# Moving two thirds of the float64 weight conversions from the expert stage into the gated passes of a fused attention, expert and gated-network kernel

## The chip, the cores and the metric

The kernel runs on one core of a Trainium2 chip. The metric is the device time of one execution in microseconds (us). The engines of the core are named as the profile names them: PE (TensorE, matrix products), DVE (VectorE), ACT (ScalarE), POOL (GpSimd) and SP (SyncE, which only issues DMAs here). Each works through its own instructions in order, and semaphores tie them together.

## The reference

Attention over eight batches of eight heads in two directions (x reads the state, the state reads x) gives 8 x 544 = 4352 tokens of width 512. A router with capacity 544 assigns each token to one of eight experts, greedily over all sorted logits. Each expert is relu(x w1) w2 with 1024 hidden columns. A gated network follows.

```python
logits = x @ w_gate
order = np.argsort(-logits.flatten())      # greedy, at most N // E tokens per expert
for e in range(E):
    mask = assigned == e
    h = np.maximum(x[mask] @ w1[e], 0.0)
    out[mask] = h @ w2[e]
...
g = x @ w_gate                             # moe2: 512 x 1536
silu = g * (1.0 / (1.0 + np.exp(-g)))
val = x @ w_val                            # moe2: 512 x 1536
return (silu * val @ w_out).astype(np.float32)   # moe2: 1536 x 512
```

The three weights of the gated network, w_gate, w_val and w_out, arrive as float64.

## The kernel before

Four stages follow one another: attention with the first search of the router (0 to about 188 us), the experts (to about 690), two gated passes (to about 1207) and the output products (to the end). All large products are made of float32 values that are split in two parts, hi (rounded, by ACT) and lo (the rest, by DVE), and each product takes the three combinations that matter.

**Experts.** There are 128 units u, 16 per expert: two parts of its 544 tokens (matmuls of 256 and of 288 columns) times eight blocks of hidden columns. A unit is `hidden` (L789: 12 matmuls into a bank h, then relu on ACT at L802 and its rest on DVE at L803) and, one unit later, `expert_out` (L806: 12 matmuls, L813, L814, L817). The weights of the next expert come meanwhile: four DMAs of 512 KB for w1 (L734) and four for w2 (L739) on SP's queue, then split on ACT (L725) and DVE (L726). The router's search for the next expert runs in between, as a chain of small DVE and PE instructions. What is done ahead of which unit is written out by hand: `at(u, hook, f, ...)` puts a call in front of unit u, and a hook places the instructions of that call behind a named instruction on that instruction's engine only. The hooks 'h' and 'hh' are the last L803 (DVE) and the last L802 (ACT).

**Conversions.** Float64 weights become float32 in 36 steps. `load64(n)` (L158) brings 512 KB of raw float64 into a buffer raw64 (two buffers), with ACT issuing the DMA (L167). `convert(n)` (L170) is one ACT multiply (L175) into mag, three DVE instructions (L177, L178, L180) into f32v and a store of 256 KB to v_d (L181, SP). Step n stands for (j, q, u): six blocks j of hidden columns, q = gate, val, out, and two halves u. All 36 stand in the experts (L991): the load in front of unit 10 + 3.2 n, behind hook 'hh', the conversion 3 units later, with hook 'h'.

**Gated passes.** The gated products are made by a seven-product scheme over 2x2 blocks (the order of the products is PORDER = 1, 6, 7, 5, 2, 4, 3). Operands are sums and differences of blocks: POOL makes four of them per operand (`s_sums` L860, `t_sums` L870, instructions L864 to L867 and L876 to L879, tiles tt out of six buffers), and ACT and DVE split them (`split`, L841 and L842). With a key, `keep` (L849) stores the four sums in DRAM, and a later call with that key loads them (`kept`, L854). Each of the two passes p goes over nine groups n of tokens (index 4 is a small group of leftovers), three units jj each (L1159). A unit has 84 matmuls (L1044; 48 in the small group), reads out of banks b1 to b4 (two buffers each) by ACT (L1075) and DVE (L1078 and others), gating (L1051 to L1053), and a store of m (L1096). A pass needs the split weights of three blocks j. In pass 0, further work is written behind units of the groups: the sums of w3, w4, w5 (`pair_load`, `pair_sums`) and of w_out o0, o1, o2 (`out_load`, `out_sums`), stored for later. In pass 1 the first six sums of activations (`acts_load`, `acts_sums`, keys a0 to a5, EARLY = 6) are made and stored.

**Output.** 27 steps, each a seven-product update with w_out (L1231); the sums of the next step's activations are loaded if they were stored, or made on POOL.

Of the kernel before, what the change touches and what calls it, by code (L numbers as in the profile page):

```python
# [21 lines left out]
F32 = mybir.dt.float32  # L22
# [3 lines left out]
I32 = mybir.dt.int32  # L26
# [9 lines left out]
E = 8  # L36
# [5 lines left out]
NT = 5  # L42
NW = 24
NY = (8, 6)
EARLY = 6
P_ = {'spin': 12, 'xl': 2, 'pc': (0, 9), 'ct': 12, 'cuts': (0, 34), 'lead': [0, 1, 10, 25, 44, 57, 73, 89], 'hook': ['p', 'p', 'p', 'p', 'p', 'x', 'p', 'p'], 'w': [8, 14, 8, 8, 8, 8, 8, 8], 'whook': 'h', 'g': [0, 3, 18, 36, 56, 70, 85, 103], 'gs': 0.34, 't': [0, 14, 29, 46, 61, 75, 91, 104], 'ts': 1, 'ghook': 'p', 'thook': None, 't0': (2, 4, 5), 'l0': 10, 'lp': 3.2, 'cd': 3, 'lhook': 'hh', 'chook': 'h', 'swap': [], 'y0': 16, 'f0': [10, 4, 3]}
PRE = 24
HEAD = "z0 m0 f0 p l z1 m1 x0 x3 x2 e0 f1 x1 e1 q"
ORDER = "z0 f0 p t0 t1 z1 G l m0 f1 x0 m1 r0 x1 s0 e0 r1 x2 x3 r2 s1 k e1 c q r3"
# [8 lines left out]
def moe_kernel(ctx: ExitStack, tc: tile.TileContext, x, state, moe_w_gate, moe_w1, moe_w2,  # L58
               moe2_w_gate, moe2_w_val, moe2_w_out, out):
    nc = tc.nc  # L60
# [64 lines left out]
    for q in range(2):  # L125
        pair = []
        for part in "hl":
            t = ac.tile([128, 4, 128], FR, name=f"SB{part}{q}")
# [3 lines left out]
    for q in range(3):  # L132
        pair = []
        for part in "hl":
            t = ac.tile([128, 2, 4, ROW], FR, name=f"RB{part}{q}")
# [19 lines left out]

    raw64 = {}

    def load64(n):  # L158
        j, q, u = n // 6, n // 2 % 3, n % 2
        src = (moe2_w_gate, moe2_w_val, moe2_w_out)[q]  # L160
        if q < 2:
            src_u = src[256 * u:256 * u + 256, 256 * j:256 * j + 256]
        else:
            src_u = src[256 * j + 128 * u:256 * j + 128 * u + 128]
        k = 2 if q < 2 else 1
        raw64[n] = bw.tile([128, 512, 2], I32, name="raw64", bufs=2)
        nc.scalar.dma_start(raw64[n].rearrange("p (k f) w -> p k (f w)", k=k),  # L167
                            src_u.bitcast(I32).rearrange("(k p) f -> p k f", p=128))

    def convert(n):  # L170
        j, q, u = n // 6, n // 2 % 3, n % 2
        raw = raw64.pop(n)
        low, top = raw[:, :, 0], raw[:, :, 1]
        mag = bw.tile([128, 512], F32, name="mag", bufs=1)
        nc.scalar.mul(mag, top.bitcast(F32), 2.0 ** -112)  # L175
        v = bw.tile([128, 512], I32, name="f32v", bufs=1)
        nc.vector.tensor_scalar(v, low, 29, None, op0=OP.logical_shift_right)  # L177
        nc.vector.scalar_tensor_tensor(v, mag.bitcast(I32), 3, v,  # L178
                                       op0=OP.logical_shift_left, op1=OP.bitwise_or)
        nc.vector.scalar_tensor_tensor(v, top, -2**31, v, op0=OP.bitwise_and, op1=OP.bitwise_or)  # L180
        nc.sync.dma_start(v_d[j, q][:, u], f32(v))  # L181
# [411 lines left out]
    for b in range(B + 1):  # L593
        steps = ORDER if 0 < b < B else HEAD if b == 0 else TAIL
        for op in steps.split():
            k, q = op[0], int(op[1:] or 0)
# [243 lines left out]
    def split(hi, lo, src):  # L840
        nc.scalar.copy(hi, src)  # L841
        nc.vector.tensor_tensor(lo, src, f32(hi), OP.subtract)  # L842

    def tmp(pool):
        return pool.tile([128, 2, 256], F32, name="tt", bufs=4 if pool is bw else 6)

# [39 lines left out]
    def pair_load(j, pool):  # L886
        if pool is bw:
            raws = [pool.tile([128, 1024], F32, name="raw", bufs=4) for _ in range(2)]
        else:
            raw = pool.tile([128, 2048], F32, name="raw", bufs=2)  # L890
            raws = [raw[:, :1024], raw[:, 1024:]]
        for q in range(2):
            nc.sync.dma_start(raws[q], v_d[j, q].rearrange("p u f -> p (u f)"))
        if pool is bw:
            parts = [r.rearrange("p (q u k f) -> p q u k f", q=1, u=2, k=2) for r in raws]
        else:
            parts = [raw.rearrange("p (q u k f) -> p q u k f", q=2, u=2, k=2)]
        return [[v[:, :, u, :, 128 * i:128 * i + 128] for i in range(2) for u in range(2)] for v in parts]

    def pair_sums(A, pool, key=None):  # L900
        cut = [lambda t, q=q: t.rearrange("p q (k f) -> p q k f", k=2)[:, q:q + 3 - len(A)] for q in range(len(A))]
        if key in sums_d:
            S1, S2, S3, S4 = kept(key, pool)
        else:
            S1, S2, S3, S4 = S = s_sums(A, pool, cut)
            if key:
                keep(key, S)
        whole = lambda t: [c(t) for c in cut]
        return {1: [a[0] for a in A], 6: whole(S2), 7: whole(S3), 2: [a[1] for a in A],
                5: whole(S1), 4: [a[3] for a in A], 3: whole(S4)}  # L910
# [77 lines left out]
            at(P_["t"][k] + int(j * P_["ts"]), P_["thook"], turn, k, j)  # L988
    for j in range(2, NT):
        at(P_["t0"][j - 2], "p", turn, 0, j)  # L990
    for n in range(36):  # L991
        at(int(P_["l0"] + P_["lp"] * n), P_["lhook"], load64, n)
        at(int(P_["l0"] + P_["lp"] * n + P_["cd"]), P_["chook"], convert, n)

    pend = None
    for u in range(16 * E):
        i, hf, f = u // 16, u // 8 % 2, u % 8
# [105 lines left out]
    def acts_load(gi, jj):  # L1103
        n = 4 if gi < E else 2
        raw = cw.tile([128, 2048], F32, name="raw", bufs=2)[:, :512 * n].rearrange("p (r i t) -> p r i t", r=2, i=n)
        nc.sync.dma_start(raw, m_d[gi][:, 2 * jj:2 * jj + 2])
        return raw

    def acts_sums(gi, raw, key=None):
        if gi < E:  # L1110
            a11, a21, a12, a22 = (raw[:, :, i] for i in range(4))
            if key in sums_d:
                S1, S2, S3, S4 = kept(key, cw)
            else:
                S1, S2, S3, S4 = S = s_sums([(a11, a12, a21, a22)], cw, [lambda t: t])
                if key:
                    keep(key, S)
            return {1: a11, 6: S2, 7: S3, 2: a12, 5: S1, 4: a22, 3: S4}
        a1, a2 = raw[:, :, 0], raw[:, :, 1]
        t, neg = tmp(cw), tmp(cw)  # L1120
        nc.gpsimd.tensor_tensor(t, a1, a2, OP.add)
        nc.gpsimd.tensor_scalar(neg, a1, -1.0, None, op0=OP.mult)
        return {1: a1, 2: a2, 3: t, 7: neg}
# [6 lines left out]
    def out_load(jj):  # L1130
        raw = cw.tile([128, 2048], F32, name="raw", bufs=2).rearrange("p (r i f) -> p r i f", r=2, i=2)
        for r in range(2):
            nc.sync.dma_start(raw[:, r], v_d[2 * jj + r, 2])
        return raw

    def out_sums(jj, raw):
        return t_sums([raw[:, :, i, 256 * d:256 * d + 256] for i in range(2) for d in range(2)], cw, f"o{jj}")
# [21 lines left out]
    for p, n, gi, jj in hidden_units:  # L1159
        nxt = groups[p][n + 1] if n < E else None  # L1160
        if jj == (p == n == 0) and nxt is not None:
            ysrc = y_sums(nxt, y_load(nxt, cw), cw)

        def after(step):
            if nxt is None or (gi == E) != (step < 3 and gi == E):
                return
            if gi == E:
                todo = {(0, 1): (0, 1), (0, 2): (1, 2), (1, 1): (2, 3), (1, 2): (3, 4), (2, 1): (4, 5), (2, 2): (5, 7)}
                a, b = todo[jj, step]
                todo = PORDER[a:b]  # L1170
            else:
                todo = {(1, 1): (1,), (1, 7): (6,), (1, 5): (7,), (2, 1): (5,), (2, 6): (2,), (2, 2): (4,),
                        (2, 5): (3,)}.get((jj, step), ())
            for m in todo:
                if m in ysrc:
                    y_combo((p, nxt), m, ysrc)

        if n == E and p == 0 and jj == 0:
            wraw = pair_load(3, cw)
        unit(key, 3 * p + jj, gi, after)  # L1180
        if p == 1 and 2 <= n < 2 + EARLY and n < E:
            if jj == 1:
                early = acts_load(*outs[n - 2])
            elif jj == 2:
                acts_sums(outs[n - 2][0], early, f"a{n - 2}")
        if p == 0 and 1 <= n < 7 and jj == 1:
            early = pair_load(n + 2, cw) if n < 4 else out_load(n - 4)
        if p == 0 and 1 <= n < 7 and jj == 2:
            if n < 4:
                pair_sums(early, cw, f"w{n + 2}")  # L1190
            else:
                out_sums(n - 4, early)
        if n == E and p == 0:
            src = pair_sums(wraw, cw, f"w{3 + jj}")
            if jj < 2:
                wraw = pair_load(4 + jj, cw)
            for m in PORDER:
                pair_combo(3 + jj, m, src)
        if n == E and p == 1:
            src = out_sums(jj, out_load(jj))  # L1200
            for m in PORDER:
                out_combo(jj, m, src)
            if jj == 1:
                acts[0] = acts_sums(outs[0][0], acts_load(*outs[0]), "a0")
                acts_prep(0, slice(0, 7))
        if jj == 2 and nxt is not None:
            key = (p, nxt)
        elif jj == 2 and p == 0:
            key = (0, gi)
# [101 lines left out]
```

## Time and profile before

| | us |
|---|---|
| median of three runs | 1485.01 |
| lowest and highest | 1481.55, 1488.06 |
| the profiled execution | 1485.12 |
| its span, first to last instruction | 1483.5 |
| PE busy (matmuls) | 1384.4 |
| DVE busy | 1126.4 |
| ACT busy | 571.0 |
| POOL busy | 468.2 |

Busy times are those of the profiled execution. Matmuls are pipelined, so a PE that is busy all the time can still wait a little inside. Views used below: the chain of work that ended last, busy times of each engine in given stretches, waits of an engine by what ended them, and instructions in order of time. The granted clock is the share of full speed that TensorE was given in a stretch; it has two levels, 1.0 (2.4 GHz) and 0.5 (1.2 GHz).

### The profile page before, as it was taken

To read this page: it belongs to the slowest core of one execution; us is meant where nothing else is said; L and a number is where in the kernel's file an instruction comes from. 1 tells how busy PE (TensorE), PEld (TensorE's weight loads), DVE (VectorE), ACT (ScalarE), POOL (GpSimd) and SP (SyncE) were. 2 spreads that over 40 slices of the span, in tenths; PEclk is the share of its full clock that TensorE was granted. 3 is DMA by queue.
4 is the path that set the end of the run, shared out by engine and by line. 5 is a ranking of instruction groups with operands and counts; after the bars stand their busy time and mean duration, and the time that the engine had idled before them with its cause. 6 is when DMAs were issued, how large, how long until landed. Compare 5 with 4: busy or idle time off the path is not lost.

```text
span 1483.5 us, 29094 instructions
## 1 busy us (share of the span) xinstructions
PE 1384.4 (93%) x11440; PEld 1335.4 (90%) x11441; DVE 1126.4 (76%) x2152; ACT 571.0 (38%) x1124; POOL 468.2 (32%) x398
## 2 busy tenths in 40 slices
PE   6998389998999999999999999999999999999997
PEld 5776278988988899999999999999999999999996
DVE  5898768876777765586888677976856797999982
ACT  5885124332332333343323232522323264444441
POOL 4775331100111001152553410012131002778872
PEclk9999579999999999999999999999999999999999
DMA  7542225545444356455665553635465378334431
GB/s 129 124 113 91 97 77 192 188 155 192 147 163 160 126 197 213 164 181 199 225 237 192 192 185 115 234 143 192 173 213 204 129 246 294 119 138 144 151 118 43
DMA packets 125417, 244.67 MB, mean 165 GB/s; under 512 B 48096, under 2 KB 57312, under 8 KB 118624
## 3 DMA queue, kind: packets, MB, share of 16 engines
q1 hardware_dynamic: 107696, 203.46, 40.6%
q10 hardware_dynamic: 11472, 19.43, 4.2%
q0 software_dynamic: 6112, 19.93, 3.9%
q8 instruction: 89, 1.46, 0.4%
q14 instruction: 48, 0.39, 0.1%
HBM read 157.84 MB, written 84.93 MB: 164 GB/s over the span
## 4 chain that ended last, share of the span: by engine, by line
PE 71%; DVE 11%; DMA 8%; issue 4%; ACT 3%; POOL 2%; SPq 0%; POOLq 0%; DVEq 0%; ACTq 0%
PE b L1044 44%; PE h L798 11%; PE y L817 4%; PE y L813 4%; PE y L814 3%; DMA raw<-in_moe_w_out_dram 2%; DMA raw<-v_d 1%; DMA raw<-in_moe_w_gate_dram 1%; DMA raw<-in_moe_w_val_dram 1%; DVE w L726 1%; PE bt L777 1%; DMA xc<-in_x_dram 1%; DVE xw L320 1%; DVE yb L842 1%; DMA raw<-in_moe_w_dram 1%
## 5 line engine op out<-in xcount | busy, mean ns | idle before, releaser
L1044 PE MATMUL b<-yb,w 128*128 128x256 f32 x4320 | 517.5, 282 | 6.9 <-DVE cs L1084 5.7
L1044 PEld LDWEIGHTS b<-yb,w 128*128 128x128 f32 x4320 | 515.0, 190 | 9.3 <-DVE cs L1084 7.2
L1044 PE MATMUL b<-w,yb 128*128 128x256 f32 x2160 | 257.2, 282 | 0.0
L1044 PEld LDWEIGHTS b<-w,yb 128*128 128x128 f32 x2160 | 257.0, 190 | 0.0
L798 PE MATMUL h<-xh,w 128*128 128x288 f32 (+1 forms) x1024 | 215.4, 303 | 0.7 <-issue 0.7
L798 PEld LDWEIGHTS h<-xh,w 128*128 128x128 f32 x1024 | 167.8, 197 | 1.7 <-issue 1.1
L768 POOL DMA_INDIRECT xg<-xm_d,idx x38 | 48.1, 1265 | 367.8 <-PE bt L777 163.4
L842 DVE TENSOR_TENSOR yb<-tt,yb 128x512 fp32r<-128x512 f32 x164 | 143.7, 893 | 14.4 <-ACT yb L841 14.4
L813 PE MATMUL y<-hh,w 128*128 128x288 f32 (+1 forms) x512 | 140.2, 300 | 12.6 <-DVE ys L825 4.8
L798 PE MATMUL h<-xl,w 128*128 128x288 f32 (+1 forms) x512 | 151.9, 299 | 0.0
L841 ACT CAST yb<-tt 128x512 fp32r<-128x512 f32 x164 | 101.2, 620 | 104.6 <-PE b L1044 87.8
L814 PE MATMUL y<-hh,w 128*128 128x288 f32 (+1 forms) x512 | 139.2, 298 | 0.0
L842 DVE TENSOR_TENSOR yb<-raw,yb 128x512 fp32r<-128x512 f32 x127 | 126.0, 1000 | 15.8 <-ACT yb L841 13.5
L864 POOL TENSOR_TENSOR tt<-raw 128x512 f32<-128x512 f32 (+1 forms) x33 | 42.0, 1277 | 286.9 <-DMA raw<-m_d 212.9
L802 ACT ACTIVATE hh<-h 128x288 fp32r<-128x288 f32 (+1 forms) x128 | 50.7, 397 | 199.2 <-PE h L798 177.5
L813 PEld LDWEIGHTS y<-hh,w 128*128 128x128 f32 x512 | 98.7, 194 | 14.9 <-ACT ys L823 6.3
L803 DVE SCALAR_TENSOR_TENSOR hl<-h,hh 128x288 fp32r<-128x288 f32 (+1 forms) x128 | 55.5, 435 | 69.6 <-ACT hh L802 63.7
L841 ACT CAST yb<-raw 128x512 fp32r<-128x512 f32 x127 | 78.1, 620 | 63.5 <-PE b L1044 50.2
L798 PEld LDWEIGHTS h<-xl,w 128*128 128x128 f32 x512 | 99.5, 196 | 0.2
L814 PEld LDWEIGHTS y<-hh,w 128*128 128x128 f32 x512 | 98.7, 194 | 0.3
L817 PE MATMUL y<-hl,w 128*128 128x288 f32 (+1 forms) x512 | 94.9, 300 | 2.2 <-DVE hl L803 2.2
L726 DVE TENSOR_TENSOR w<-raw,w 128x1024 fp32r<-128x1024 f32 x61 | 73.8, 1238 | 16.1 <-ACT w L725 15.4
(253 smaller groups left out, 2107.7 us busy)
## 6 DMA issues: line engine op xcount, KB each, us to landing
raw<-in_moe_w_dram SPq DMA_DIRECT2D x60, 512.0 KB
raw<-m_d SPq DMA_DIRECT2D x30, 1024.0 KB
m_d<-m SPq DMA_DIRECT2D x48, 512.0 KB
raw<-v_d SPq DMA_DIRECT2D x32, 512.0 KB
raw<-y_d SPq DMA_DIRECT2D x14, 1024.0 KB
v_d<-f32v SPq DMA_DIRECT2D x36, 256.0 KB
xm_d<-xm SPq DMA_DIRECT2D x8, 1024.0 KB
y_d<-ys SPq DMA_DIRECT2D x16, 512.0 KB
```

The source lines that it names most:

```text
L726: eng.tensor_tensor(lo, raw, f32(hi), OP.subtract)
L768: hooks["g"] = nc.gpsimd.indirect_dma_start(out=xg[:n], out_offset=None, in_=xm_d, in_offset=bass.IndirectOffsetOnAxis(ap=idx[i][:n, j:j + ...
L798: hooks["p"] = nc.tensor.matmul(ph, W[i][0][k][q == 1][:, fs], (xl if q == 2 else xh)[:, k, :T], start=(n == 0), stop=(n == 11)).ins
L802: relu[16 * i + 8 * hf + f] = hooks["hh"] = nc.scalar.activation(hh, ph, AF.Relu).ins
L803: hooks["h"] = nc.vector.scalar_tensor_tensor(hl, ph, 0.0, f32(hh), op0=OP.max, op1=OP.subtract).ins
L813: nc.tensor.matmul(p[d], wh[:, f % 2, ds_], hh, start=(f == 0), stop=False)
L814: nc.tensor.matmul(p[d], wl[:, f % 2, ds_], hh, start=False, stop=False)
L817: nc.tensor.matmul(p[d], wh[:, f % 2, ds_], hl, start=False, stop=(f == 7))
L841: nc.scalar.copy(hi, src)
L842: nc.vector.tensor_tensor(lo, src, f32(hi), OP.subtract)
L864: nc.gpsimd.tensor_tensor(S1, a21, a22, OP.add)
L1044: nc.tensor.matmul(p[:, q], a(x, q), b(y), skip_group_check=True, start=start and not (q or n or m), stop=stop and q == 1 and n == last an ...
```

## The change

The order of the 36 conversions becomes a list CONV: first the 12 for the gate and val weights of j = 0 to 2, then the 12 for those of j = 3 to 5, then the 12 for w_out. The experts keep the first 12, one every 8.4 units, each conversion 6 units behind its load. The second 12 are written into pass 0, the third into pass 1: with group n the load of one behind unit 0, the load of a second and the conversion of the first behind unit 1, the conversion of the second behind unit 2, in six groups of each pass (n = 0, 1, 2, 3, 5, 6). Their loads are issued by SP, raw64 there has one buffer, and mag and f32v are taken from the six tt buffers. The sums of w3, w4, w5 move from groups 1, 2, 3 of pass 0 to groups 2, 5, 7; those of w_out from groups 4, 5, 6 of pass 0 to groups 2, 5, 7 of pass 1. Of the activations' sums four are made ahead and stored instead of six, at groups 1, 3, 4, 6 of pass 1.

```diff
-EARLY = 6
-P_ = {..., 'lp': 3.2, 'cd': 3, ...}
+EARLY = 4
+P_ = {..., 'lp': 8.4, 'cd': 6, ...}
...
-    def load64(n):
-        j, q, u = n // 6, n // 2 % 3, n % 2
+    CONV = ([(j, q, u) for j in range(3) for q in range(2) for u in range(2)]
+            + [(j, q, u) for j in range(3, 6) for q in range(2) for u in range(2)]
+            + [(j, 2, u) for j in range(6) for u in range(2)])
+
+    def load64(n, pool=None, eng=nc.scalar):
+        j, q, u = CONV[n]
...
-        raw64[n] = bw.tile([128, 512, 2], I32, name="raw64", bufs=2)
-        nc.scalar.dma_start(raw64[n].rearrange("p (k f) w -> p k (f w)", k=k),
+        raw64[n] = (pool or bw).tile([128, 512, 2], I32, name="raw64", bufs=1 if pool else 2)
+        eng.dma_start(raw64[n].rearrange("p (k f) w -> p k (f w)", k=k),
...
-    def convert(n):
-        j, q, u = n // 6, n // 2 % 3, n % 2
+    def convert(n, pool=None):
+        j, q, u = CONV[n]
...
-        mag = bw.tile([128, 512], F32, name="mag", bufs=1)
+        mag = bw.tile([128, 512], F32, name="mag", bufs=1) if pool is None else flat(tmp(pool))
...
-        v = bw.tile([128, 512], I32, name="f32v", bufs=1)
+        v = bw.tile([128, 512], I32, name="f32v", bufs=1) if pool is None else flat(tmp(pool)).bitcast(I32)
...
-    for n in range(36):
+    for n in range(12):
         at(int(P_["l0"] + P_["lp"] * n), P_["lhook"], load64, n)
         at(int(P_["l0"] + P_["lp"] * n + P_["cd"]), P_["chook"], convert, n)
...
         unit(key, 3 * p + jj, gi, after)
-        if p == 1 and 2 <= n < 2 + EARLY and n < E:
+        a = {1: 0, 3: 1, 4: 2, 6: 3}.get(n) if p else None
+        if a is not None:
             if jj == 1:
-                early = acts_load(*outs[n - 2])
+                early = acts_load(*outs[a])
             elif jj == 2:
-                acts_sums(outs[n - 2][0], early, f"a{n - 2}")
-        if p == 0 and 1 <= n < 7 and jj == 1:
-            early = pair_load(n + 2, cw) if n < 4 else out_load(n - 4)
-        if p == 0 and 1 <= n < 7 and jj == 2:
-            if n < 4:
-                pair_sums(early, cw, f"w{n + 2}")
+                acts_sums(outs[a][0], early, f"a{a}")
+        c = 12 + 12 * p + 2 * (0, 1, 2, 3, 9, 4, 5, 9, 9)[n]
+        if c < 24 + 12 * p:
+            if jj < 2:
+                load64(c + jj, cw, nc.sync)
+            if jj:
+                convert(c + jj - 1, cw)
+        k = {2: 0, 5: 1, 7: 2}.get(n)
+        if k is not None and jj == 1:
+            early2 = out_load(k) if p else pair_load(3 + k, cw)
+        if k is not None and jj == 2:
+            if p:
+                out_sums(k, early2)
             else:
-                out_sums(n - 4, early)
+                pair_sums(early2, cw, f"w{3 + k}")
```

## Rows read from the trace of the kernel before

**Rows 1.** The chain that ended last, shares of the span by engine and line.

```profile
PE b L1044 44%; PE h L798 11%; PE y L817 4%; PE y L813 4%; PE y L814 3%; DMA raw<-in_moe_w_out_dram 2%; DMA raw<-v_d 1%; DMA raw<-in_moe_w_gate_dram 1%; DMA raw<-in_moe_w_val_dram 1%; DVE w L726 1%; PE bt L777 1%; DMA xc<-in_x_dram 1%; DVE xw L320 1%; DVE yb L842 1%; DMA raw<-in_moe_w_dram 1%
```

**Rows 2.** Stretches: length, busy PE, PEld, DVE, ACT, POOL, clock, DMA share, GB/s.

```profile
244.00:690.00 446.00, 421.79 (x3682) 403.56 (x3683) 322.88 (x802) 155.09 (x300) 66.24 (x60) 0.97 0.51 169
690.00:720.00 30.00, 26.75 (x214) 26.48 (x213) 20.88 (x34) 14.49 (x26) 14.41 (x8) 0.94 0.68 246
720.00:840.00 120.00, 118.42 (x994) 117.81 (x993) 98.37 (x138) 36.58 (x65) 54.12 (x38) 1.00 0.59 214
840.00:950.00 110.00, 108.84 (x908) 107.90 (x908) 83.34 (x128) 37.25 (x66) 12.89 (x9) 1.00 0.47 166
950.00:1207.00 257.00, 256.11 (x2154) 255.71 (x2153) 192.02 (x302) 86.00 (x154) 34.37 (x25) 1.00 0.53 185
...
1244.00:1470.00 226.00, 226.00 (x1903) 226.00 (x1902) 188.36 (x200) 95.01 (x155) 162.70 (x110) 1.00 0.38 131
```

**Rows 3.** Waits of ACT from 244 to 690: total us, times, longest us.

```profile
ACT mag L175 <- DMA raw<-in_moe_w_val_dram: 21.6, 7, 8.0
ACT mag L175 <- DMA raw<-in_moe_w_out_dram: 18.4, 9, 4.7
...
ACT mag L175 <- DMA raw<-in_moe_w_gate_dram: 13.6, 5, 5.9
```

**Rows 4.** ACT in order of time, 417 to 432: start, duration, instruction, [idle before].

```profile
420.76 0.37 ACTq L167 DMA_DIRECT2D raw<-in_moe_w_val_dram  x1
429.20 0.66 ACT L175 ACTIVATE mag<-raw 128x512 f32<-128x512 f32 x1 [8.03 <-DMA raw<-in_moe_w_val_dram]
429.76 0.40 ACT L802 ACTIVATE hh<-h 128x288 fp32r<-128x288 f32 x1
```

**Rows 5.** SP's DMA issues in order of time, same stretch.

```profile
418.12 4.04 SPq L739 DMA_DIRECT2D raw<-in_moe_w_dram  x4
```

**Rows 6.** One stretch of 2 us while these transfers run, columns as in rows 2.

```profile
426.00:428.00 2.00, 2.00 (x25) 1.74 (x24) 0.65 (x2) 0.00 (x0) 0.00 (x0) 1.00 1.01 373
```

**Rows 7.** Stretches around nine idle times of PE in the experts, and their sum.

```profile
302.00:306.00 4.00, 3.00 (x32) 2.76 (x31) 2.51 (x6) 2.40 (x4) 1.07 (x1) 1.00 0.81 249
338.00:342.00 4.00, 2.61 (x22) 2.40 (x21) 0.64 (x5) 0.86 (x3) 2.90 (x3) 1.00 0.90 298
363.00:376.00 13.00, 10.47 (x95) 9.49 (x93) 5.51 (x14) 3.36 (x5) 0.00 (x0) 0.74 0.34 114
...
616.00:625.00 9.00, 6.63 (x40) 6.05 (x39) 2.94 (x5) 2.96 (x6) 0.00 (x0) 0.81 0.47 168
...
sum 72.00, PE 52.60 PEld 48.45 DVE 32.24 ACT 22.25 POOL 10.01; mean PE 5.84 PEld 5.38 DVE 3.58 ACT 2.47 POOL 1.11
```

**Rows 8.** A conversion's DVE instructions: duration ns min/median/max, first and last start.

```profile
L177 DVE TENSOR_SCALAR f32v<-raw x36: 413/419/1158, 250.8 to 679.6; 128x512 int32<-128x512 int32 x36
L178 DVE SCALAR_TENSOR_TENSOR f32v<-mag,f32v x36: 669/685/1660, 251.3 to 680.2; 128x512 int32<-128x512 int32 x36
L180 DVE SCALAR_TENSOR_TENSOR f32v<-raw,f32v x36: 668/688/1111, 252.6 to 681.2; 128x512 int32<-128x512 int32 x36
```

**Rows 9.** Groups by line: count, busy us, mean ns, idle before and its releasers.

```profile
L842 DVE TENSOR_TENSOR yb<-tt,yb 128x512 fp32r<-128x512 f32 x164 | 143.7, 893 | 14.4 <-ACT yb L841 14.4
...
L1078 DVE TENSOR_TENSOR u<-b,s 128x512 f32<-128x512 f32 x48 | 32.8, 684 | 4.0 <-PE b L1044 3.5
```

**Rows 10.** SP and ACT in order of time, 722 to 790, one row each.

```profile
736.71 1.59 SPq L893 DMA_DIRECT2D raw<-v_d  x2
...
768.39 0.58 ACT L1075 COPY s<-b 128x512 f32<-128x512 f32 x1
```

**Rows 11.** From the chain (start, us, what) and from PE in time.

```profile
697.32 7.95 DMA raw<-y_d
...
715.05 1.20 PE L1044 MATMUL b<-yb,w 128*128 128x256 f32 x8 [3.25 <-DVE cs L1084]
```

More of the change, by code (lines that the diff above doesn't have):

```diff
@@ L44 @@
 NY = (8, 6)
-EARLY = 6
-P_ = {'spin': 12, 'xl': 2, 'pc': (0, 9), 'ct': 12, 'cuts': (0, 34), 'lead': [0, 1, 10, 25, 44, 57, 73, 89], 'hook': ['p', 'p', 'p', 'p', 'p', 'x', 'p', 'p'], 'w': [8, 14, 8, 8, 8, 8, 8, 8], 'whook': 'h', 'g': [0, 3, 18, 36, 56, 70, 85, 103], 'gs': 0.34, 't': [0, 14, 29, 46, 61, 75, 91, 104], 'ts': 1, 'ghook': 'p', 'thook': None, 't0': (2, 4, 5), 'l0': 10, 'lp': 3.2, 'cd': 3, 'lhook': 'hh', 'chook': 'h', 'swap': [], 'y0': 16, 'f0': [10, 4, 3]}
+EARLY = 4
+P_ = {'spin': 12, 'xl': 2, 'pc': (0, 9), 'ct': 12, 'cuts': (0, 34), 'lead': [0, 1, 10, 25, 44, 57, 73, 89], 'hook': ['p', 'p', 'p', 'p', 'p', 'x', 'p', 'p'], 'w': [8, 14, 8, 8, 8, 8, 8, 8], 'whook': 'h', 'g': [0, 3, 18, 36, 56, 70, 85, 103], 'gs': 0.34, 't': [0, 14, 29, 46, 61, 75, 91, 104], 'ts': 1, 'ghook': 'p', 'thook': None, 't0': (2, 4, 5), 'l0': 10, 'lp': 8.4, 'cd': 6, 'lhook': 'hh', 'chook': 'h', 'swap': [], 'y0': 16, 'f0': [10, 4, 3]}
 PRE = 24
@@ L842, in split, with flat @@
         nc.vector.tensor_tensor(lo, src, f32(hi), OP.subtract)
+    def flat(t):
+        return t.rearrange("p a b -> p (a b)")
     def tmp(pool):
```

## Prediction

> **What bounds the kernel now.** I read the chain that ended last first, then the busy times by stage, and then I followed the one stage that is not full of matmuls. The chain [rows 1] is TensorE's (PE's) for the most part: L1044 (gated passes and output products) alone is 44% of it. But it runs through three DMAs of raw float64 weights, in_moe_w_out, in_moe_w_gate and in_moe_w_val, 2%, 1% and 1% of the span. Those are the loads of the conversions that the change moves, and a transfer on the chain means that something in front of PE waited for it.
>
> The stages [rows 2] say where. From 690 us to the end PE is busy 118.4 of 120, 108.8 of 110, 256.1 of 257 and 226.0 of 226 us: nothing can be won there. In the experts, 244 to 690, it is busy 421.8 of 446, and its mean granted clock is 0.97 instead of 1.00. So 24 us of idle time and about 0.03 x 446 = 13 us of lost clock are the whole pool.
>
> The mechanism is ScalarE's (ACT's) queue. ACT waits 21.6 + 18.4 + 13.6 = 53.6 us for those loads, in 21 waits, the longest 8.0 us, always at L175, the multiply of a conversion [rows 3]. One of them close up [rows 4]: the load is issued at 420.76, the multiply stands right behind it in ACT's queue, it starts at 429.20 after 8.03 us of idle ACT, and the relu of the next expert unit (L802) stands behind the multiply and starts at 429.76. PE ran out of work meanwhile. Why the load took so long: four weight tiles of 512 KB were issued by SyncE (SP) from 418.12 on [rows 5], and while they and the raw load run the 16 DMA engines are busy 1.01 of the time at 373 GB/s [rows 6].
>
> I then took a stretch around each of the nine places where PE ran dry behind such a wait [rows 7]. The sum row covers all nine: idle PE is 72.0 - 52.6 = 19.4 us. After five of them, from 363 on, the granted clock also fell to its lower level (0.5, that is 1.2 GHz). Length times (1 - clock) is what that cost: 13 x 0.26 = 3.4 us in the first of the five, 9 x 0.19 = 1.7 in the last, 11.9 over the five. Together 31.3 us of the pool of 37 stand behind the conversions. That is the ceiling of this change.
>
> **Part 1: 24 of 36 conversions leave the experts.** What stays is n = 0 to 11, loaded at units 10, 18, 26, 35 and so on, one every 8.4 units. The text puts the conversion 6 units behind its load instead of 3, but the hook of a conversion is a VectorE (DVE) instruction, so it holds the three DVE instructions only. The multiply on ACT is not held: in the unit shown it is placed 3 units behind its load by the text and ran right behind it [rows 4]. So I do not expect the wider distance to remove waits by itself; what removes them is that there are a third as many loads. Nine in 36 loads led to a stretch like those of [rows 7], at 31.3 / 9 = 3.5 us each. At the same rate 12 loads give 3 stretches, 10.4 us, a gain of 31.3 - 10.4 = 20.9 us. If only the two loads that keep their unit (26 and 35, the first two of the nine stretches, before 302 and 338 us) still lead to one, 7 us remain at the mean price, or 2.4 at their own, since they lost 1.0 + 1.4 us of PE and no clock [rows 7], and the gain is 24 to 29 us. DVE gets 24 x 1.79 = 43 us lighter here (0.419 + 0.685 + 0.688, the medians of [rows 8]) of 322.9 busy us [rows 2], and less raw traffic stands beside the expert weights; this helps the same waits. I take **-25 us**, bounds -32 and -19.
>
> **Part 2: they arrive in the gated passes.** Each brings a 512 KB load, now on SP's queue, one ACT multiply, three DVE instructions and a 256 KB store on SP. ACT is busy 36.6 of 120 and 86.0 of 257 us [rows 2], and every product has two PSUM buffers, so PE runs up to a unit, 84 x 226.0 / 1903 = 10 us, ahead of ACT and DVE: an ACT wait of the sizes of [rows 3] is hidden as long as DVE can catch up. DVE can in pass 1: 192.0 of 257 us busy, and 12 x 1.79 = 21 us more makes 213. Over pass 0 it can as well, 20.9 + 98.4 + 83.3 = 202.6 of 260. The first 120 us cannot take all 12: 98.4 busy leaves 21.6 us. Nothing ties a gated conversion to the group in which it is written, and the order shows that such work is drawn forward: the load for the sums of w4 is written behind the second unit of the third group, whose first ACT copy (L1075) is at 768.39, and it is issued at 736.71 [rows 10]. Limits are one buffer of raw64 and two spare buffers of tt, so I expect nearly all 12 in the first 120 us.
>
> What one costs there depends on GpSimd (POOL), busy 54.1 of 120 us with sums. An instruction that reads two SBUF tiles, like the split L842, averages 893 ns, the addition L1078, one of whose inputs is in PSUM, 684 ns for the same 128x512 [rows 9]; L178 and L180 are of the first kind and reach 1660 and 1111 ns against medians of 685 and 688 [rows 8]. A conversion that meets POOL costs up to 1.158 + 1.660 + 1.111 = 3.9 us; at POOL's share of 45% I take 0.55 x 1.79 + 0.45 x 3.3 = 2.5 us. Twelve are 30 us, and 98.4 + 30 is 8 us over 120. Three of the 14 stored or direct sums of pass 0 go to pass 1 (those of w_out), which gives some of this back. **+5 us**, bounds 0 and +12.
>
> The Trainium skill (SBUF — State Buffer, "Who interferes with whom") speaks against this part: it says that a DVE instruction with two SBUF inputs and a GpSimd instruction that reads SBUF exclude each other for the whole instruction, so work moved from a stage with POOL at 66 of 446 us to one at 54 of 120 grows. The 893 against 684 ns agree with it. By that rule alone, an estimate, each of the two instructions would wait half a POOL sum in 45% of the cases; without it the 12 would cost 21.5 us and just fit.
>
> **Part 3: the way into pass 0.** PE's last idle time of size, 3.25 us before 715.05, hangs on the load of y for the second group, 7.95 us long [rows 11]. The first raw load of the gated passes is written ahead of it on the same queue. 0.5 MB more at the 214 to 246 GB/s that this stretch moves [rows 2] is some 2 us. **+2 us**, bounds 0 and +4. On SP's queue a load of the second raw tile of a group waits for the DVE instructions of the first; the store of m and the stores of sums stand behind it. DVE does these in the same order as SP, so this adds little as long as part 2 holds.
>
> **Part 4: four stored sums of rows instead of six.** Eight tiles of sums fewer are stored and loaded again; in the output products POOL makes them instead, 8 x 162.7 / 110 = 12 us. There PE is busy 226.0 of 226 us with POOL at 162.7 [rows 2] in just this pattern, so the cost is 0; without that cover 2 us.
>
> **The sum.** -25 + 5 + 2 + 0 = -18 us against the profiled execution, 1485.1 us (span 1483.5), which is also the median of the runs, 1485.0. Predicted **1467 us**. A measurement of this kernel tells about 0.5%, 7.4 us, from no change.
>
> **The rivals.** (a) Still behind the bursts: the multiply stays glued to its load and the 12 loads left meet the weight bursts more often than 1 in 4, say half of them. Then 6 x 3.5 = 21 us stay and 10 are gained, and with +7 the time is 1482, no change. For it: rows 4 and 5; against it: the loads that remain have more DMA time around them. Chance 0.17. (b) All hidden: DVE's spare time in pass 0 is found where it lies, and only the two old places lose time; with some of the small waits gone too, -32 + 0 + 1, 1454. Chance 0.16. (c) Slower: pass 0 becomes DVE's. If pass 1's 12 conversions are drawn forward too, DVE has 98.4 + 83.3 = 181.7 us from 720 to 950 and gets 24 x 3.0 = 72 more, 254 in 230 us; PE loses 24, the experts win 15, the way in costs 2: 1496. It decides from the point at which DVE has more than 118 us of work in 120. This is also where the rule cited from the Trainium skill in part 2 would lead if every conversion met a POOL sum. For it: [rows 10]; against it: the two spare buffers of tt. Chance 0.12. The forecast keeps 0.55.
>
> **Range and chances.** (b) and the good end of the forecast reach down to 1450; the bad end, -19 + 12 + 4, is 1482, and (a) lies there too. 1450 to 1483 leaves out (c) and a little more. Faster by over 0.5%: 0.72 (forecast, (b)); within: 0.17; slower: 0.11.
>
> **What would show it.** Right: the waits of L175 for raw loads in the experts down to a third or less, PE's idle time there under 12 us, the clock at 0.99; DVE at 95% or more from 720 to 840 and PE short of full there by some microseconds; the output products as before. Wrong in part 1: the chain still passes through raw loads as often as now. Wrong in part 2: PE full in pass 0 ((b)), or idle for tens of microseconds with DVE full ((c)).

## The result, and the profile after

The changed kernel takes 1467.7 us (median of 8 runs, 1461.4 to 1471.1), the kernel before 1481.4 us (8 runs, 1473.9 to 1488.1): a ratio of 0.990, 95% interval 0.988 to 0.993. Its profiled execution took 1470.5 us, with a span of 1468.9 against 1483.5. So it is faster by about 14 us, and the time lies on the forecast of 1467 us. How it came about does not hold as well. The stage lengths below are taken from the start of the first matmul of a stage to that of the next, and for the output products to the start of their last matmul (pass 1 begins with the 2161st L1044, L1051 after the change; measured so, the passes of the kernel before end at 1215.5 us and not at about 1207).

| us | before | after | difference | forecast |
|---|---|---|---|---|
| experts | 502.9 | 469.3 | -33.6 | -25 (-32 to -19) |
| pass 0 | 265.9 | 274.9 | +9.0 | +7 (0 to +16) |
| pass 1 | 258.3 | 268.0 | +9.7 | 0 |
| output products | 256.7 | 256.7 | 0.0 | 0 |
| span | 1483.5 | 1468.9 | -14.6 | -18 |

The experts gave more than the bounds allowed, pass 1 took what nothing was set aside for, and the two misses, -8.6 and about +12, nearly cancel. The stages of the changed kernel, and last the stretch that the forecast named, with the columns of [rows 2]:

```profile
244.00:657.00 413.00, 410.10 (x3686) 394.68 (x3686) 283.62 (x734) 141.46 (x276) 62.35 (x60) 1.00 0.42 138
658.00:933.00 275.00, 261.06 (x2163) 258.43 (x2162) 227.05 (x344) 100.68 (x180) 62.61 (x41) 0.99 0.59 205
933.00:1201.00 268.00, 259.43 (x2162) 257.28 (x2162) 218.04 (x339) 91.09 (x162) 42.56 (x29) 1.00 0.63 223
1201.00:1457.00 256.00, 256.00 (x2155) 256.00 (x2154) 213.68 (x238) 111.15 (x183) 175.09 (x118) 1.00 0.41 143
...
720.00:840.00 120.00, 112.78 (x927) 111.42 (x927) 98.56 (x150) 37.93 (x68) 38.80 (x25) 0.99 0.62 215
```

In the experts PE is idle for 2.9 us where it was for 24, at a granted clock of 1.00 instead of 0.97 [rows 2]. In the passes it is idle 13.9 + 8.6 us, and DVE, which the forecast had as the cause, is busy 227 of 275 and 218 of 268 us, about 82% in both. From 720 to 840, where the forecast looked for 95% or more, it is busy 82% too, as it was before [rows 2]; eight of the twelve conversions of pass 0 start there, where nearly all were expected. What PE waited for in the passes, after the change (658 to 1201; total us, times, longest):

```profile
PE b L1051 <- DVE cs L1091: 14.7, 15, 3.0
PE b L1051 <- ACT s L1082: 4.9, 2, 2.7
PE b L1051 <- DVE u L1085: 2.9, 4, 1.2
```

The longest of these in the kernel before (691 to 1215; L1084 there is L1091 here), where all of them came to 6.6 us:

```profile
PE b L1044 <- DVE cs L1084: 5.7, 5, 3.2
```

The waits of ACT show why its reading and DVE's come late; the first two rows are of the experts, 244 to 657, the others of the passes, 658 to 1201 (L179 is the multiply, mag its result in the experts, tt in the passes).

```profile
ACT mag L179 <- DMA raw<-in_moe_w_val_dram: 13.7, 5, 6.0
ACT mag L179 <- DMA raw<-in_moe_w_gate_dram: 4.6, 4, 2.1
...
ACT tt L179 <- DMA raw<-in_moe_w_out_dram: 22.3, 8, 6.1
ACT tt L179 <- DMA raw<-in_moe_w_gate_dram: 8.1, 4, 3.8
ACT tt L179 <- DMA raw<-in_moe_w_val_dram: 6.8, 2, 5.9
```

Of the 53.6 us of such waits in the experts [rows 3] 18.3 are left there, and 37.2 us stand in the passes. Here is one, on ACT, DVE and PE from 816 to 829.

```profile
824.47 0.66 ACT L179 ACTIVATE tt<-raw 128x512 f32<-128x512 f32 x1 [5.86 <-DMA raw<-in_moe_w_val_dram]
...
825.17 0.43 DVE L181 TENSOR_SCALAR tt<-raw 128x512 int32<-128x512 int32 x1 [4.45 <-DMA v_d<-tt]
825.52 0.69 DVE L1088 TENSOR_TENSOR u<-b,u 128x512 f32<-128x512 f32 x1
...
827.46 1.82 PE L1051 MATMUL b<-yb,w 128*128 128x256 f32 x13 [3.01 <-DVE cs L1091]
```

ACT and DVE both stand still, at the two instructions of one conversion that read the same raw tile: ACT's multiply for the raw load, DVE's first shift (L181) until 0.7 us after the multiply began. The shift needs the raw load as well, which had landed by then; the last 0.7 us are by the profile those of the store of an earlier conversion, which frees its tt buffer. (Over the passes, L181 waits 9.9 us in 7 waits for raw loads and 5.9 us in 3 for such stores.) The readings of PE's banks, L1088 and L1091, are queued behind; PE's next product adds to the bank that L1091 reads, and PE is idle for 3.0 us. DVE is not full, it is blocked.

### The profile page after: what moved, and what is told of

It reads as the page before. It is cut to its first block, busy times and chain, and to the rows that moved or that the text cites. A ratio compares the mean times of both kernels' runs of the same rounds, so it can differ in the third digit from the quotient of the medians.

```text
span 1468.9 us, 29080 instructions
## 1 busy us (share of the span) xinstructions
PE 1375.8 (94%) x11441; PEld 1326.9 (90%) x11441; DVE 1130.6 (77%) x2152; ACT 569.7 (39%) x1124; POOL 465.9 (32%) x398
## 4 chain that ended last, share of the span: by engine, by line
PE 68%; DVE 15%; issue 6%; DMA 5%; ACT 3%; POOL 2%; SPq 0%; POOLq 0%; DVEq 0%; ACTq 0%
PE b L1051 36%; PE h L802 13%; PE y L821 4%; PE y L817 4%; PE y L818 4%; DVE yb L846 2%; PE bt L781 1%; DVE m L1059 1%; DVE u L1088 1%; DMA xc<-in_x_dram 1%; DVE w L846 1%; DVE tt L184 1%; DVE u L1085 1%; DMA v_d<-tt 1%; DMA raw<-in_moe_w_out_dram 1%
## 5 line engine op out<-in xcount | busy, mean ns | idle before, releaser
L1051 PE MATMUL b<-yb,w 128*128 128x256 f32 x4320 | 520.5, 282 | 22.5 <-DVE cs L1091 14.7
L1051 PEld LDWEIGHTS b<-yb,w 128*128 128x128 f32 x4320 | 515.6, 190 | 27.3 <-DVE cs L1091 17.9
L1051 PE MATMUL b<-w,yb 128*128 128x256 f32 x2160 | 257.2, 282 | 0.0
L1051 PEld LDWEIGHTS b<-w,yb 128*128 128x128 f32 x2160 | 257.0, 190 | 0.0
L802 PE MATMUL h<-xh,w 128*128 128x288 f32 (+1 forms) x1024 | 211.9, 299 | 0.7 <-ACT xh L786 0.7
L802 PEld LDWEIGHTS h<-xh,w 128*128 128x128 f32 x1024 | 164.6, 193 | 1.6 <-ACT xh L786 1.1
L817 PE MATMUL y<-hh,w 128*128 128x288 f32 (+1 forms) x512 | 137.1, 294 | 0.8 <-DVE ys L829 0.8
L846 DVE TENSOR_TENSOR yb<-raw,yb 128x512 fp32r<-128x512 f32 x127 | 125.3, 996 | 14.9 <-ACT yb L845 14.7
L818 PE MATMUL y<-hh,w 128*128 128x288 f32 (+1 forms) x512 | 135.9, 292 | 0.0
L817 PEld LDWEIGHTS y<-hh,w 128*128 128x128 f32 x512 | 96.8, 190 | 1.5 <-ACT hh L806 1.0
L818 PEld LDWEIGHTS y<-hh,w 128*128 128x128 f32 x512 | 96.8, 190 | 0.1
L1058 ACT ACTIVATE m<-cs 128x768 f32<-128x768 f32 x48 | 40.6, 846 | 117.0 <-DVE cs L1100 116.8
```

The lines of the kernel that those rows point to most:

```text
L802: hooks["p"] = nc.tensor.matmul(ph, W[i][0][k][q == 1][:, fs], (xl if q == 2 else xh)[:, k, :T], start=(n == 0), stop=(n == 11)).ins
L817: nc.tensor.matmul(p[d], wh[:, f % 2, ds_], hh, start=(f == 0), stop=False)
L818: nc.tensor.matmul(p[d], wl[:, f % 2, ds_], hh, start=False, stop=False)
L1051: nc.tensor.matmul(p[:, q], a(x, q), b(y), skip_group_check=True, start=start and not (q or n or m), stop=stop and q == 1 and n == last an ...
L1058: nc.scalar.activation(m, g, AF.Sigmoid)
```

## Experiments

Each run below changes one thing (both_held the same thing in two places). Stage lengths are read as above, each from one profile; a table at the end has them all. Where a ratio is given, it comes from four to six executions of the run and seven to ten of the kernel before; the other runs were executed once. Two profiles of the same kernel (after and changed_again, all_36_held and all_36_again) differ by up to 2.4 us in a stage, and four_sums below differs from the kernel before by 3.1 and 5.0 us in stages that its edit leaves alone, so a difference of that size in one profile shows nothing by itself.

**No conversions in the passes.**

```diff
+    zero64 = cw.tile([128, 512], F32, name="zero64")
+    nc.gpsimd.memset(zero64, 0.0)
...
-            if jj < 2:
-                load64(c + jj, cw, nc.sync)
             if jj:
-                convert(c + jj - 1, cw)
+                j64, q64, u64 = CONV[c + jj - 1]
+                nc.sync.dma_start(v_d[j64, q64][:, u64], zero64)
```

> The changed kernel without the work of its 24 gated conversions: no raw load, no multiply, no DVE instruction; their stores stay and write zeros, so the output is that of other weights. In the changed kernel the two passes take 274.9 and 268.0 us, before 266.0 and 258.2. If the conversions themselves are what the passes pay for (by whichever mechanism), the passes come back to 266 and 258 within 2 us and the span from 1468.9 to about 1450. Rival: the moved sums and the reloads at the ends of the passes are what costs; then both passes stay above 270 and 264.

Measured: passes 264.9 and 258.6, span 1450.0. The loss of the passes is that of the conversions written into them; the moved sums and reloads cost nothing that shows.

**One raw load in each pass.**

```diff
             if jj < 2:
-                load64(c + jj, cw, nc.sync)
+                if c + jj in (12, 24):
+                    load64(c + jj, cw, nc.sync)
+                    once = raw64[c + jj]
+                raw64[c + jj] = once
```

> The changed kernel with one raw load in each pass instead of 12: all 12 conversions of a pass read that tile, so multiply, DVE instructions, stores and tt buffers stay as they are and only the waits for raw loads and 12 MB of traffic go; the weights are wrong. Theory 1, the passes lose time because ACT's multiply and DVE's first shift stand in their queues waiting for a raw load: passes together back from 542.9 to 530 us or less (before 524.2), span 1456 or less. Theory 2, DVE has 24 conversions more work beside GpSimd and that is the loss, as the prediction had it for pass 0: passes stay at 538 or more, span 1464 or more.

Measured: passes 271.2 + 262.9 = 534.1, span 1461.4. That is between the two: about half of the 18.7 us go with the loads. The two largest of the things that the multiply still waits for in the passes are these.

```profile
ACT tt L179 <- POOL tt L874: 5.9, 1, 5.9
ACT tt L179 <- DVE tt L182: 5.4, 2, 3.3
```

No raw load is left in the list, but with its data at hand the multiply is drawn still further forward (that of the eighth conversion of pass 0 starts at 741.1 us, in the changed kernel at 759.7), and now it stands in the queue for one of the six tt buffers, held by a sum or by an earlier conversion. So the load alone is not the whole cost; the next run takes away the standing in the queues itself.

**The gated conversions held.** The multiply is bound to come after the last sigmoid of the unit behind which it is written, the DVE instructions after its last gating product.

```diff
-        nc.scalar.activation(m, g, AF.Sigmoid)
+        hooks["sig"] = nc.scalar.activation(m, g, AF.Sigmoid).ins
...
-        nc.vector.tensor_tensor(m, v, m, OP.mult)
+        hooks["gv"] = nc.vector.tensor_tensor(m, v, m, OP.mult).ins
...
-                convert(c + jj - 1, cw)
+                with tc.issue_after(hooks["sig"]), tc.issue_after(hooks["gv"]):
+                    convert(c + jj - 1, cw)
```

> The changed kernel with each gated conversion held behind the last sigmoid (ACT) and the last gating product (DVE) of the unit behind which it is written, so a raw load has about one unit (10 us) to land before anything stands in a queue for it; all the work stays. Theory 1 (waiting in the queue): passes 530 us or less together, the waits of the multiply under 8 us instead of 37, ratio to the kernel before 0.980 to 0.984. Theory 2 (DVE's work): passes 540 or more, ratio 0.989 as for the changed kernel.

Measured: passes 264.9 + 264.0 = 528.9, ratio 0.986 (0.980 to 0.991; a little above the 0.980 to 0.984 expected), span 1455.7. Of the multiply's waits in the passes this is the whole list:

```profile
ACT tt L179 <- DMA raw<-in_moe_w_out_dram: 0.8, 2, 0.5
ACT tt L179 <- DMA raw<-in_moe_w_gate_dram: 0.6, 1, 0.6
```

The work is the same, 24 conversions on DVE in the same passes, at 2.3 us each (L181, L182 and L184 average 464, 701 and 1100 ns; in the changed kernel it was 2.4), and 14.0 of the 18.7 us are gone. So standing in the queues was about three quarters of the cost. What is left for DVE's work is 4.7 us here and 1.9 us in both_held below, no more than two profiles can differ by. Both engines are held at once, so how much is due to the multiply on ACT and how much to the shift on DVE is not shown.

**All 36 in the experts, the multiply held.** The kernel before, with one edit.

```diff
+    def held(n):
+        with tc.issue_after(hooks["hh"]):
+            convert(n)
+
     for n in range(36):
...
-        at(int(P_["l0"] + P_["lp"] * n + P_["cd"]), P_["chook"], convert, n)
+        at(int(P_["l0"] + P_["lp"] * n + P_["cd"]), P_["chook"], held, n)
```

> The kernel before, all 36 conversions in the experts, with one thing changed: the multiply of a conversion is held on ACT behind the relu of the unit in front of which the conversion is written, three units behind its load, as the three DVE instructions are held already. Theory 1: the stretches in which PE runs dry behind a raw load vanish without moving any work; the experts go from 502.9 to 470 to 480 us, the passes stay at 524, ratio 0.977 to 0.985. Rival: the number of conversions (DVE time, raw traffic beside the expert weights) is what the experts pay for; then the experts stay above 495 us and the ratio above 0.993.

Measured: experts 470.4, passes 266.6 + 258.2, ratio 0.984 (0.978 to 0.989), span 1448.9. ACT in order of time around one load:

```profile
409.41 0.37 ACTq L167 DMA_DIRECT2D raw<-in_moe_w_val_dram  x1
413.67 0.41 ACT L802 ACTIVATE hh<-h 128x288 fp32r<-128x288 f32 x1 [3.85 <-PE h L798]
...
422.67 0.66 ACT L175 ACTIVATE mag<-raw 128x512 f32<-128x512 f32 x1
```

The stage of that run, with the columns of [rows 2]:

```profile
244.00:655.00 411.00, 406.71 (x3656) 390.65 (x3654) 319.19 (x795) 154.49 (x300) 65.19 (x60) 1.00 0.54 181
```

It is the load of [rows 4], n = 15. Its multiply comes 13 us later with no idle time before it, relus pass in between, and each of them waits for PE only. DVE does all the conversions and is busy 319 of 411 us, and the DMA engines are as loaded as before, yet PE is idle for 4.3 us and the clock is at 1.00. So neither DVE's time nor the traffic was what the conversions cost the experts, but for a few microseconds (both_held below). It was the multiply in ACT's queue.

**The distance back to 3 units** (the changed kernel with 'cd': 3 for 'cd': 6).

> The changed kernel with the conversions in the experts written 3 units behind their loads, as before, instead of 6. If the distance holds only the DVE instructions, and the multiply on ACT stands right behind its load anyway, nothing moves: the multiply's waits for raw loads stay near the 19.7 us of the changed kernel, the experts take 467 to 473 us (469.3 in the changed kernel). Rival: the longer distance is what gave the loads their time; then the waits grow past 30 us and the experts take 476 us or more.

Measured: experts 470.9, waits of the multiply for raw loads 11.3 + 2.4 = 13.7 us in the experts (18.3 in the changed kernel, same stretch), span 1468.1. The longer distance does nothing for the multiply.

**The loads every 8.0 units instead of 8.4** ('lp': 8.0).

> The changed kernel with the 12 loads in the experts one every 8.0 units instead of 8.4. The number stays 12, but now every second load stands at unit 16 m + 10, one or two units behind the four w2 loads of an expert, where in the changed kernel only those at units 10 and 26 do. If the place beside the weight loads decides, the four new ones (42, 58, 74, 90) cost as the load at unit 26 does, and as the nine stretches of the kernel before did, some 3.5 us each: waits of the multiply 35 us or more, experts 480 to 486 us. Rival, the number of loads decides (3.5 us for a quarter of them, as the prediction reckoned): experts 467 to 473 us.

Measured: experts 489.5, above the 480 to 486 expected, span 1484.6. The same 12 conversions at other places cost 20 us more, 5 us for each of the four new meetings where 3.5 was reckoned, and the gain over the kernel before is gone. The chain of that run from 244 to 670 goes through five raw loads, at units 26, 42, 58, 74 and 90, each right behind the w2 loads of an expert (in the changed kernel through one, at unit 26). Two of the five:

```profile
356.29 7.52 DMA raw<-in_moe_w_gate_dram
418.41 7.93 DMA raw<-in_moe_w_val_dram
```

The multiply of the second of these, at unit 58, on ACT in order of time:

```profile
426.42 0.66 ACT L179 ACTIVATE mag<-raw 128x512 f32<-128x512 f32 x1 [7.61 <-DMA raw<-in_moe_w_val_dram]
```

**The same places, the multiply held** ('lp': 8.0 and the edit of all_36_held in the changed kernel).

> The same loads every 8.0 units, with the multiply held on ACT behind the relu in front of which the conversion is written, six units behind its load. If a load beside the weights costs only through the multiply that stands in ACT's queue, the place no longer matters: no wait of the multiply over 1 us, experts 464 to 470 us. Rival: the raw load also delays the weights themselves (it shares the DMA engines with them); then the experts stay within 4 us of the run without the hold.

Measured: experts 465.9, no wait of the multiply left in them, span 1457.6. Held, the bad places are as good as the others. A raw load beside the weights does not hold up the weights in a way that PE sees.

**Four stored sums alone** (the kernel before with EARLY = 4).

> The kernel before with four stored sums of activations instead of six, and nothing else (they are made at groups 2 to 5 of pass 1). The prediction had this part at 0: output products 256.7 us as before, passes 524 us together, experts 502.9 within 3. Rival: GpSimd's 8 sums more beside the output products slow DVE's splits enough to stall PE; then the output products take 258.5 us or more.

Measured: output products 256.7, experts 499.8, span 1479.4. The experts lie 3.1 us from the kernel before, a little outside the 3 expected. Pass 1 took 256.9, pass 0 270.9, 5.0 us longer than before, with two waits of PE for ACT in it, 4.7 us together; the edit touches only pass 1 and what follows, so the cause of this stays open. The stored sums are worth nothing either way in the output products.

**Side by side**, six executions of each. First the changed kernel, then all 36 held, then the changed kernel with both edits (held in the experts and in the passes).

> The changed kernel once more, on the same chip as the two below: ratio 0.990 to the kernel before, passes 543 us together, experts 469.

Measured: 0.991 (0.988 to 0.994), experts 467.9, passes 541.9.

> The kernel before with all 36 conversions in the experts and their multiply held, as in the run all_36_held, to set it beside the changed kernel: theory 1 (the wait in ACT's queue is the whole cost of the conversions in the experts) has it at 0.983, some 10 us faster than the changed kernel, since it pays nothing in the passes. Rival: its lead was a matter of that chip; then the two lie within 0.3% of each other.

Measured: 0.982 (0.979 to 0.985), 1456.8 us; experts 471.9, passes 526.1.

> The changed kernel with its multiplies held in both places: in the experts behind the relu in front of which the conversion is written, in the passes behind the sigmoid and the gating product of the unit. No wait of a multiply for a raw load is left. Theory 1: experts 465 to 470 us, passes 529 as in gated_held, span 1451 to 1457, ratio 0.982 to 0.986; that is no better than with all 36 held in the experts, because 24 conversions still take DVE's time in the passes. Rival: fewer conversions help the experts by themselves; then the experts take 462 us or less and the ratio is under 0.981.

Measured: 0.979 (0.976 to 0.982), 1452.1 us, experts 467.2, passes 264.5 + 261.6 = 526.1, span 1451.0. This is the fastest version. The ratio lies below the 0.982 to 0.986 expected, and the clause "no better than all 36 held" was wrong by 4.6 us, the difference of the medians. Its experts and its passes:

```profile
244.00:656.00 412.00, 411.10 (x3706) 395.64 (x3705) 285.82 (x736) 142.23 (x279) 63.93 (x60) 1.00 0.42 139
656.00:1182.00 526.00, 516.78 (x4321) 514.61 (x4320) 447.41 (x681) 188.53 (x342) 102.33 (x70) 1.00 0.62 220
```

PE is idle for 0.9 of 412 us in the experts and for 9.2 us in the passes (22.5 in the changed kernel). Moving the conversions, once nothing stands in a queue for them, is worth 4.6 us in the medians; the profiles put it in the experts, 471.9 and 467.2 (470.4 in all_36_held), and in the passes it costs nothing that shows, 526.1 in both.

| run | experts | pass 0 | pass 1 | span |
|---|---|---|---|---|
| before | 502.9 | 265.9 | 258.3 | 1483.5 |
| after | 469.3 | 274.9 | 268.0 | 1468.9 |
| changed_again | 467.9 | 276.3 | 265.6 | 1465.3 |
| no_gated_conv | 471.7 | 264.9 | 258.6 | 1450.0 |
| one_load_a_pass | 472.7 | 271.2 | 262.9 | 1461.4 |
| gated_held | 469.6 | 264.9 | 264.0 | 1455.7 |
| all_36_held | 470.4 | 266.6 | 258.2 | 1448.9 |
| all_36_again | 471.9 | 267.6 | 258.5 | 1455.2 |
| distance_3 | 470.9 | 276.2 | 267.3 | 1468.1 |
| every_8_units | 489.5 | 275.1 | 266.0 | 1484.6 |
| bursts_held | 465.9 | 274.9 | 265.0 | 1457.6 |
| four_sums | 499.8 | 270.9 | 256.9 | 1479.4 |
| both_held | 467.2 | 264.5 | 261.6 | 1451.0 |

The spans carry some microseconds of the stages ahead of the experts as well, which no run changed (the experts begin between 183.6 and 189.1 us).

## Why the prediction was right and where it was wrong

**What bounds the kernel** was right. The nine stretches of [rows 7] were worth 31.3 us by their idle time and clock; all_36_held, which takes away nothing but the wait, gives 502.9 - 470.4 = 32.5 us. As "the ceiling of this change" 31.3 was too low: the change gained 33.6 us in the experts, nearly all of the pool of 37, so the idle time outside the nine stretches went with them.

**Part 1, -25, measured -33.6, outside its bounds.** That the distance of 6 units would not help was right (distance_3). The step that failed is "At the same rate 12 loads give 3 stretches". It treated the meeting of a raw load with a weight burst as a matter of how many loads there are. It is a matter of where they stand: w2 is always loaded near unit 16 m + 8, and a raw load at 16 m + 10 is behind it. Of the 12 loads of the changed kernel only units 10 and 26 stand there, and one stretch is left, a wait of 6.0 us at unit 26, with 2.0 us of idle PE and a clock of 0.83 from 298 to 308. With 8.0 for 8.4, six of 12 stand there and the experts take 489.5. That one constant is worth more than the whole change. The second load that the forecast kept, at unit 35, cost nothing: it now stands some 10 us behind the w1 loads instead of right behind them, and from 335 to 349 PE is busy all the time at a clock of 1.00.

**Part 2, +5, measured +9.0 and +9.7 (with part 3).** The size for pass 0 came out near, the mechanism did not. The step that failed is "every product has two PSUM buffers, so PE runs up to a unit, 84 x 226.0 / 1903 = 10 us, ahead of ACT and DVE", and with it "an ACT wait of the sizes of [rows 3] is hidden as long as DVE can catch up" and the whole reckoning by DVE's busy time. Within a unit three of the four banks are filled twice: b1 by products 1 and 2, b2 by 6 and 4, b4 by 5 and 3. The second product cannot start before the first has been read, by L1082, L1085 and L1091, and these are the three lines that PE waited for, 4.9 + 2.9 + 14.7 = 22.5 us, 20.4 of it right ahead of a product that fills its bank for the second time. Between the two products stand 36 matmuls for b1 and b2 and 24 for b4, by the prediction's own rate an estimate of 4.3 and 2.9 us. That is all that PE can run on, and a stop of ACT and DVE of 4 to 6 us is longer.

How both engines come to stop at once was overlooked too. The prediction saw that nothing ties a gated conversion to its group, but drew from it only that the conversions come early. The hook that held the DVE instructions in the experts is missing in the passes, so both the multiply and the first shift can stand right behind the load. In pass 1 this holds as much as in pass 0, hence 9.7 us where 0 was written. The row of the kernel before that should have warned is [rows 4]: the same multiply, in the same kind of place.

**DVE's longer instructions** were sized well but hardly mattered. In the passes L181, L182 and L184 average 490, 818 and 1072 ns, 2.4 us a conversion against the 2.5 assumed. That is longer than the medians of [rows 8]. The Trainium skill (SBUF — State Buffer, "Who interferes with whom") says that a DVE instruction with two SBUF inputs contends with a GpSimd instruction that reads SBUF. The trace agrees: of the 48 L182 and L184 in the passes, the 26 that no POOL instruction overlaps take 0.67 to 0.69 us, and the 17 that take over 1.1 us, up to 1.79, all overlap one. But gated_held does nearly all of this work and is 4.7 us from the kernel before in 24 conversions, both_held shows nothing against all_36_again. The prediction's rival (c) stood on this mechanism, and its price of 24 us for the passes was not far from the 18.7 measured, for another reason.

**Part 3, +2**, cannot be seen: PE's idle time ahead of the second group is 2.1 us now (it was 3.25, [rows 11]). **Part 4, 0**, was right: output products 256.7 us in both, in four_sums too; POOL is busy 175 us in them after the change for 163 before, the 12 us more that were reckoned.

**The sum.** -33.6 + 18.7 makes -14.9 where -18 was written. The time was right by luck: two errors of about 10 us lay on opposite sides, and the remaining 3 to 4 us were made up by the base, since the kernel before has a median of 1481.4 us over eight executions and not the 1485.0 of the first three. Rival (a), with its 1482, was no idle worry: with the spacing at 8.0 instead of 8.4 the kernel took 1486.2 us, against 1482.8 for the kernel before beside it, one execution each.

## What to carry to other kernels

When an instruction waits for a DMA, look at what stands behind it in its own queue. An order that is placed "as soon as the data should be there" makes every late transfer a stall of the whole engine; binding the instruction behind one that comes a DMA's time later cost nothing that shows and was worth more here than moving two thirds of the work. A hook holds only the engine whose instruction it names: check each engine that the step uses. Two buffers of a bank do not let PE run ahead past a place where the same buffer is filled a second time. And before a gain is put down to having less of something, move it by a few slots: here the same 12 conversions took 20 us more by their places alone.

## What the runs showed that was not expected

A DMA of 512 KB that is issued behind 2 MB of others took some 6 to 8 us until its user could start (7.61 us of wait at unit 58 with loads every 8.0 units), and the same load with the same neighbours cost nothing that shows once its user came later (bursts_held): with all 36 loads in the experts, DMA traffic at 0.54 of the 16 engines left PE idle 1% of the time (all_36_held).
